# Sliding-window attention with slot experts: keys in blocks of 64 that meet 96 queries, TensorE in program order

## The chip, the cores and the metric

The kernel runs on one core of a Trainium2 chip. The metric is the device time of one execution in microseconds; the median over runs is compared. A core has five engines that run their own queues side by side: TensorE (matmuls, with weight loads that overlap them), VectorE, ScalarE, GpSimd and SyncE. Here GpSimd and SyncE do little but issue DMA transfers. PSUM is the matmuls' output memory, eight banks of 2 KB for each of 128 partitions.

## The reference

Attention over 8 batches, 8 heads, 576 positions and 64 dimensions; four heads see the last 32 positions, four see every fourth of the last 128. The result, as 4608 rows of 512, goes through a soft mixture of 8 experts with 4 slots each.

```python
scores = scale * np.matmul(q, k.transpose(0, 1, 3, 2))
rel = pos[:, None] - pos[None, :]
mask_plain = (rel >= 0) & (rel < 32)
mask_dil = (rel >= 0) & (rel < 128) & (rel % 4 == 0)
attn = softmax(np.where(masks, scores, -1e9))
x = np.matmul(attn, v)                      # -> [4608, 512]
logits = x @ phi                            # [4608, 32]
slot_input = softmax(logits, axis=0).T @ x  # over all rows
for e in range(8):
    slot_out[e] = np.maximum(slot_input[e] @ w1[e], 0.0) @ w2[e]
out = softmax(logits, axis=1) @ slot_out
```

The softmax over all rows means that no expert can start before the last batch's attention is done.

## The kernel before

The work is cut into 32 units: batch `b` and a pair of heads, four units a batch in the order plain, dilated, plain, dilated (`unit`). A unit goes through these stages.

- `transposes` turns q and k (96 rows by 64 columns at a time, on TensorE) and copies them out of PSUM, on ScalarE into `qT` (two buffers) and `kTp`, on VectorE into `kTd` for the dilated units.
- `scores` multiplies 128 keys by 160 queries (plain) or 128 keys by 144 queries and 16 more (dilated), two heads on the two halves of the contracted rows, in two parts with a PSUM tile of two banks each.
- `softmax_parts` applies exp on ScalarE, one instruction for each part, and multiplies by a 0/1 mask on VectorE. There is no subtraction of a maximum; a column of ones in V gives the sum.
- `values` multiplies the masked exp with V, in two halves of three and two output blocks; VectorE takes a reciprocal of the sums (L399) and scales (L400) for each half.
- `x_transposes` turns the result into `xT` for the logits.

Once a batch, `select_v` (L205, L216, L225) uses matmuls with 0/1 matrices (`pick`) to bring the loaded V from "four rows to a partition" to one row to a partition; ScalarE copies the result to `vp`. `spread_v` (L194) copies the dilated V into `vd`, on VectorE. `front_logits`, `front_rows` and `front_slots` follow a batch, five to seven units later, with the logits, the exponentials by rows, and the slot sums. `last_early`, `last_logits` and `last_slots` do the last batch. Then `expert_in` (L675, ReLU L683, transposes L686) and `expert_out` (L699) take experts in pairs, `so` is copied, and eleven output tiles are computed (L735) and stored from SyncE's queue.

Loads: SyncE's queue takes the first part of q, the identity, the masks and phi; GpSimd's takes all q, k and v, converted from fp32 to fp16 on the way (`load_batch`, seven transfers a batch, all eight batches in a row), then w1 and w2 of each expert into the memory where a batch's q, k and v lay (`home0` to `home7`). So w1 of expert `e` waits until batch `e` has been read out.

Order: tiles and dependencies are tracked by a framework that orders each engine's queue by its own estimate when the program is built; only GpSimd's queue is kept as written. At run time each engine's queue is strictly in order. The calls stand like this:

```python
for u in range(NU + 5):
    st = scores(u + 1)
    values(u)
    softmax_parts(u + 1, st)
    transposes(u + 3)
    ...  # front_*, by u % 4
    x_transposes(u - 1)
    if u % 4 == 3: spread_v(u // 4 + 1); select_v(u // 4 + 1)
```

Of the kernel before, what the change touches and what calls it, by code (L numbers as in the profile page):

```python
# [15 lines left out]
B = 8  # L16
# [16 lines left out]
QW = 160  # L33
# [3 lines left out]
DW = CL + 16  # L37
# [6 lines left out]
def constants():  # L44
    j = np.arange(128)[:, None]
    i = np.arange(QW)[None, :]
    d = i - j
    keep = ((d >= 0) & (d < WINDOW)).astype(np.float16)
    m, n = np.arange(128)[:, None], np.arange(64)[None, :]
    ends = (m // 32 == n // 16) & (m % 32 <= n % 16)  # L50
    band = np.concatenate([keep, ends], axis=1).astype(np.float16)
    ident = np.eye(128, dtype=np.float16)
    return band, ident
# [3 lines left out]
def kernel(  # L57
# [11 lines left out]
    band_np, ident_np = constants()  # L69
    band_dram = nc.inline_tensor(band_np, name="band_d")  # L70
    ident_dram = nc.inline_tensor(ident_np, name="ident_d")

    consts = ctx.enter_context(tc.tile_pool(name="consts", bufs=1))
    ident = consts.tile([128, 128], FP16, name="ident")
    mask = consts.tile([128, QW + 2 * N_SLOTS + 256], FP16, name="mask")
    phi_sb = consts.tile([128, 4, N_SLOTS], FP32, name="phi_sb")
# [5 lines left out]
    nc.sync.dma_start(out=ident, in_=ident_dram.ap())  # L82
    nc.sync.dma_start(out=mask[:, 0 : QW + 64], in_=band_dram.ap())
    nc.sync.dma_start(out=phi_sb, in_=moe_phi.rearrange("(p r) s -> p r s", r=4))
# [13 lines left out]
    pick = kept([128, 4, 32, 4], "pick")  # L98
# [15 lines left out]
    Pp = kept([128, 2, NKB, 256], "Pp")  # L114
    P1 = kept([128, 2, 4, 128], "P1")
    P2 = kept([128, 2, 4, 2, 32], "P2")
# [7 lines left out]
    nc.vector.memset(Pp[:, :, :, QW:], 0.0)  # L124

    nc.vector.memset(Pp[:, :, 4, 64:QW], 0.0)
    nc.vector.memset(Pp[0:1, :, 4, 64:128], 1.0)
    nc.vector.memset(P2, 0.0)
    nc.vector.memset(P2[0:1, :, :, 0, 16:32], 1.0)
    for i in range(2):  # L130
        nc.vector.memset(vd[i][:, :, D : D + 1], 1.0)
    for i in range(NV):
# [4 lines left out]
    qT_pool = ctx.enter_context(tc.tile_pool(name="qT", bufs=2))  # L137
# [8 lines left out]
    ring = ctx.enter_context(  # L146
        tc.tile_pool(name="ring", bufs=2, space=bass.MemoryType.PSUM)
    )
    ps_o = tc.alloc_tile_pool(name="ps_o", bufs=2, space=bass.MemoryType.PSUM)
    ps_s = tc.alloc_tile_pool(name="ps_s", bufs=2, space=bass.MemoryType.PSUM)  # L150
# [3 lines left out]
    def load_batch(b):  # L154
# [15 lines left out]
        for nm, ten, hs, rows in (  # L170
# [14 lines left out]
            if nm == "kp":  # L185
                if b == 0:
                    nc.gpsimd.dma_start(out=rest[0], in_=rest[1])  # L187
                load_v("vp", 0, 4, 0, t[:, 6144:7168])
                load_v("vt", 0, 8, 512, t[96:112, 0:2048])
        load_v("vd", 4, 4, 0, t[:, 7168:8192])  # L190
# [7 lines left out]
    def select_v(b):  # L198
        raw, last = raws[b]["vp"], raws[b]["vt"]
        for i in range(2):  # L200
            sel = ps_s.tile([128, 2, 2, 4, D], FP32, name=f"sel{b}_{i}", tag="s")
            for r in range(4):
                for n in range(2):
                    rows = slice(64 * i + 32 * n, 64 * i + 32 * n + 32)
                    nc.tensor.matmul(  # L205
                        sel[:, n, 0],
                        pick[rows, r].rearrange("p i j -> p (i j)"),
                        raw[rows, :, r, :],
                        start=(r == 0),
                        stop=(r == 3),  # L210
                        tile_position=(64 * i + 32 * n, 0),
                    )
            nc.scalar.copy(out=vp[b % NV][:, 2 * i : 2 * i + 2, :, 0:D], in_=sel[:, :, 0])  # L213
        end = ring.tile([128, 2, 4, D], FP32, name=f"sel{b}_2", tag="ring")
        for r in range(4):
            nc.tensor.matmul(  # L216
                end[:, 0],
                pick[96:112, r].rearrange("p i j -> p (i j)"),
                last[:, 0:4, r, :],
                start=(r == 0),  # L220
                stop=(r == 3),
                tile_position=(96, 0),
            )
        for r in range(4):
            nc.tensor.matmul(  # L225
                end[32 * r : 32 * r + 32, 1],
                ident[96:112, 96:128],
                last[:, 4:8, r, :],
                start=True,
                stop=True,  # L230
                tile_position=(96, 32 * r),
                skip_group_check=True,
            )
        nc.scalar.copy(out=vp[b % NV][:, 4:6, :, 0:D], in_=end)
# [26 lines left out]
    def transposes(u):  # L261
        b, hp = unit(u)
        for nm in ("q", "k"):
            if nm == "q":
                dst = qT_pool.tile([128, S], FP16, name=f"qT{u}", tag="qT")
                qTs[u] = dst
            else:
                dst = kTp if hp < 2 else kTd
                kTs[u] = dst
# [30 lines left out]
    def scores(u):  # L300
        b, hp = unit(u)
        qT, kT = qTs[u], kTs[u]
        tiles = []
        for part in range(2):
            st = ps_s.tile([128, 2, 512], FP32, name=f"s{u}_{part}", tag="s")
            if hp < 2:
                todo = [(160 * i, 128 * i, 128 * i, QW) for i in range(3)] if part == 0 else [
                    (0, 384, 384, QW), (QW, 512, 512, 64)]
            else:
                todo = [(DW * cc, CL * (2 * cc + part), CL * (2 * cc + part), CL) for cc in range(2)]  # L310
                todo += [(DW * cc + CL, None, CL * (2 * cc + part) + 128, 16) for cc in range(2)]
            for at, k0, q0, n in todo:
                for g in range(2):
                    ks = q0 - 32 * g - 64 * (at // DW) if k0 is None else k0
                    nc.tensor.matmul(  # L315
                        st[:, g, at : at + n],
                        kT[64 * g : 64 * g + 64, ks : ks + 128],
                        qT[64 * g : 64 * g + 64, q0 : q0 + n],
                        start=True,
                        stop=True,  # L320
                    )
            tiles.append(st)
        return tiles

    def softmax_parts(u, tiles):
        b, hp = unit(u)
        for part in range(2):
            st = tiles[part]
            if hp < 2:
                n = (480, 224)[part]  # L330
                pr = raw_pool.tile([128, 2, n], FP16, name=f"pr{u}_{part}", tag=f"pr{part}")
                nc.scalar.activation(out=pr, in_=st[:, :, 0:n], func=AF.Exp, scale=SCALE)  # L332
                for b0, nb, w in ((0, 3, QW),) if part == 0 else ((3, 1, QW), (4, 1, 64)):
                    at = (b0 - 3 * part) * QW
                    nc.vector.tensor_tensor(  # L335
                        out=Pp[:, :, b0 : b0 + nb, 0:w],
                        in0=pr[:, :, at : at + nb * w].rearrange("p h (t c) -> p h t c", c=w),
                        in1=mask[:, None, None, 0:w].broadcast_to([128, 2, nb, w]),
                        op=ALU.mult,
                    )  # L340
                continue
            if part == 0:
                pr = dil_pool.tile([128, 2, 2, 2, DW], FP16, name=f"pd{u}", tag="pd")
            nc.scalar.activation(  # L344
                out=pr[:, part].rearrange("p c e t -> p e c t"),
                in_=st[:, :, 0 : 2 * DW].rearrange("p e (c t) -> p e c t", c=2),
                func=AF.Exp,
                scale=SCALE,
            )
        if hp < 2:  # L350
            return
        pr = pr.rearrange("p a c e t -> p a (c e) t")
        nc.vector.tensor_tensor(
            out=P1.rearrange("p a c t -> p (a c) t"),
            in0=pr[:, :, :, 0:128].rearrange("p a c t -> p (a c) t"),
            in1=mask[:, None, 0:128].broadcast_to([128, 8, 128]),
# [3 lines left out]
        nc.vector.tensor_tensor(  # L360
            out=P2.rearrange("p a c s t -> p (a c) s t")[:, :, :, 0:16],
            in0=pr[:, :, :, 128:DW].rearrange("p a c (s t) -> p (a c) s t", s=2),
            in1=mask[:, QW + 64 :].rearrange("p (c s t) -> p c s t", c=8, s=2),
            op=ALU.mult,
        )

    def values(u):
# [7 lines left out]
        for half in range(2):  # L375
            blocks = (0, 1, 2) if half == 0 else (3, 4)
            nb = len(blocks)
            ot = ps_o.tile([128, 3, 2, D + 1], FP32, name=f"o{u}_{half}", tag="o")
            mms = []
            for i, blk in enumerate(blocks):  # L380
                for h in range(2):
                    if plain:
                        P, vt = Pp, vp[b % NV]
                        mms.append((ot[:, i, h], P[:, h, blk, 0:128], vt[:, blk, hl + h, :]))
                        if blk > 0:
# [395 lines left out]
```

## Time and profile before

| | |
|---|---|
| median of 3 runs | 185.69 us (185.67 to 186.18) |
| span of the profiled execution | 183.5 us |
| TensorE busy | 151.8 us, 83% of the span |
| VectorE, ScalarE busy | 117.1 us (64%), 115.5 us (63%) |
| software DMA queue (GpSimd's) | 30.79 MB written, 93.9% of 16 engines' span |
| last weights landed | 156.74 us |
| output stored | from 158.9 us to the end |

The profile is of one execution. Busy time of an engine is the union of its instructions' times; a matmul's time includes its way through the array, so several overlap. A line of the timeline gives start, duration, engine, source line, operation, output and inputs, shapes, count, and in brackets how long the engine sat idle before it and what ended that. The clock of TensorE is recorded from 39.0 us on: full until 138.0, half until 148.2, full until 168.7, then half.

### The profile page before, as it was taken

The numbers are of one execution on the slowest core, as the hardware profiler recorded it, in microseconds if no ns is written. First come the engines' busy times: TensorE is split into PE (matmuls) and PEld (weight loads), VectorE is DVE, ScalarE is ACT, GpSimd is POOL, SyncE is SP. The second block draws the span as 40 slices with busy tenths as digits, with TensorE's granted clock in tenths as the row PEclk, the third lists the DMA queues.
The fourth block names the chain that finished last, engine by engine and source line by source line (L and its number), as shares of the span: only waits on it lengthen the run. The fifth ranks groups of instructions, "written<-read, shape, count | busy, mean of one in ns | idle before, by whom it ended". The sixth has DMA issues, their size and how long they took to land.

```text
span 183.5 us, 6054 instructions
## 1 busy us (share of the span) xinstructions
PE 151.8 (83%) x2595; PEld 105.8 (58%) x2595; DVE 117.1 (64%) x363; ACT 115.5 (63%) x208; POOL 46.9 (26%) x77
## 2 busy tenths in 40 slices
PE   1869999999988989998997998898979998885300
PEld 1637776677676667666765767666768644432000
DVE  7605886388877877878779687786970111496410
ACT  2248845689599789779878959977703022675410
POOL 7752555464554654401102001003100000000000
PEclk9999999999999999999999999999995589998555
DMA  5999999999999999999999999999999995199996
GB/s 103 183 203 203 202 203 201 202 202 204 204 201 201 204 199 204 226 211 221 212 216 216 212 216 216 218 212 218 218 214 220 212 208 105 75 440 427 427 427 262
DMA packets 23978, 41.06 MB, mean 224 GB/s; under 512 B 1680, under 2 KB 20240, under 8 KB 21136
## 3 DMA queue, kind: packets, MB, share of 16 engines
q0 software_dynamic: 21584, 30.79, 93.9%
q1 hardware_dynamic: 2368, 9.89, 13.4%
q8 instruction: 20, 0.33, 0.6%
q14 instruction: 6, 0.05, 0.1%
HBM read 62.02 MB, written 9.44 MB: 389 GB/s over the span
## 4 chain that ended last, share of the span: by engine, by line
DMA 74%; issue 15%; POOL 3%; ACT 2%; DVE 1%; PE 0%; POOLq 0%; DVEq 0%; SPq 0%
DMA home<-in_moe_w_dram 31%; DMA home<-in_v_dram 15%; DMA home<-in_k_dram 12%; DMA home<-in_q_dram 9%; DMA out_dram<-ot 7%; ACT ot L739 2%; DVE ot L741 1%; POOL home L250 1%; POOL home L162 1%; POOL home L239 1%; POOL home L184 0%; POOL home L187 0%; ACT so L716 0%; PE sop L699 0%; PE f L735 0%
## 5 line engine op out<-in xcount | busy, mean ns | idle before, releaser
L400 DVE TENSOR_TENSOR x<-o,rc 128x384 f16<-128x384 f32 x64 | 29.9, 482 | 0.5
L332 ACT ACTIVATE pr<-s 128x960 f16<-128x960 f32 (+1 forms) x32 | 24.7, 780 | 1.8 <-PE s L315 1.8
L344 ACT ACTIVATE pd<-s 128x640 f16<-128x640 f32 x32 | 20.9, 706 | 1.7 <-PE s L315 1.7
L162 POOL DMA_DIRECT2D home<-in_v_dram x24 | 16.6, 692 | 16.6 <-DMA home<-in_k_dram 11.6
L205 PE MATMUL sel<-home,pick 32*128 32x256 f16 x128 | 17.8, 307 | 1.4 <-DMA home<-in_v_dram 1.1
L399 DVE RECIPROCAL rc<-o 128x6 f32<-128x6 f32 x64 | 10.2, 177 | 13.5 <-PE o L395 13.4
L416 PE MATMUL rgx<-ident,x 128*128 128x128 f16 x160 | 15.6, 233 | 3.0 <-ACT qT L295 3.0
L741 DVE TENSOR_SCALAR ot<-f,rrow 128x512 f32<-128x512 f32 (+1 forms) x19 | 12.5, 716 | 7.7 <-DMA out_dram<-ot 5.2
L335 DVE TENSOR_TENSOR Pp<-pr,mask 128x960 f16<-128x960 f16 (+2 forms) x48 | 16.4, 394 | 0.4 <-ACT pr L332 0.4
L280 ACT COPY qT<-rgq 128x576 f16<-128x576 f16 x16 | 10.3, 641 | 9.0 <-PE rgq L275 8.5
L422 ACT COPY xT<-rgx 128x512 f16<-128x512 f16 x16 | 9.6, 601 | 10.0 <-PE rgx L416 10.0
L739 ACT ACTIVATE ot<-f,rrow 128x512 f32<-128x512 f32 (+1 forms) x19 | 11.2, 675 | 7.0 <-DMA out_dram<-ot 6.6
L239 POOL DMA_DIRECT2D home<-in_moe_w_dram x8 | 4.3, 534 | 44.4 <-PE rgq L290 36.5
L213 ACT CAST vp<-sel 128x512 f16<-128x512 f32 x16 | 9.4, 590 | 9.2 <-PE sel L205 9.0
L416 PEld LDWEIGHTS <-x 128*128 128x128 f16 x160 | 10.2, 102 | 7.2 <-issue 5.4
L735 PE MATMUL f<-so,ET 128*128 128x512 f16 (+1 forms) x38 | 11.0, 402 | 3.9 <-ACT ot L739 3.0
L275 PEld LDWEIGHTS <-home 96*64 96x64 f16 x384 | 11.9, 123 | 3.9 <-issue 2.0
L184 POOL DMA_DIRECT2D home<-in_k_dram x16 | 10.6, 661 | 10.1 <-DMA home<-in_q_dram 8.2
L395 PE MATMUL o<-vp,Pp 128*128 128x65 f16 x288 | 12.9, 203 | 0.0
L436 PE MATMUL l<-xT,phi 128*128 128x288 f16 x64 | 10.8, 304 | 2.0 <-ACT qT L280 1.7
L295 DVE COPY kTd<-rgk 128x576 f16<-128x576 f16 x16 | 12.0, 752 | 0.6 <-PE rgk L290 0.5
L295 ACT COPY qT<-rgq 128x576 f16<-128x576 f16 x16 | 10.3, 646 | 3.1 <-PE rgq L290 2.6
(105 smaller groups left out, 292.9 us busy)
## 6 DMA issues: line engine op xcount, KB each, us to landing
home<-in_moe_w_dram POOLq DMA_DIRECT2D x15, 1024.0 KB, 30.1
out_dram<-ot SPq DMA_DIRECT2D x7, 1024.0 KB, 7.5
home<-in_k_dram POOLq DMA_DIRECT2D x16, 288.0 KB, 9.9
home<-in_q_dram POOLq DMA_DIRECT2D x15, 288.0 KB, 9.7
home<-in_v_dram POOLq DMA_DIRECT2D x16, 256.0 KB, 9.8
out_dram<-ot SPq DMA_DIRECT2D x3, 512.0 KB, 6.5
home<-in_moe_w_dram POOLq DMA_DIRECT2D x2, 512.0 KB, 27.3
home<-in_v_dram POOLq DMA_DIRECT2D x8, 64.0 KB, 8.9
```

Of the source, the lines that this page charges most:

```text
L162: nc.gpsimd.dma_start(out=dst, in_=v[b, h0 : h0 + n_h, r0 : r0 + 4 * n_p, :].rearrange("h (p r) d -> p h (r d)", r=4),)
L205: nc.tensor.matmul(sel[:, n, 0], pick[rows, r].rearrange("p i j -> p (i j)"), raw[rows, :, r, :], start=(r == 0), stop=(r == 3), tile_posi ...
L275: nc.tensor.transpose(rg[64 * h : 64 * h + 64, r, :], raw[:, 2 * hp + h, D * r : D * r + D], ident[0:NP, 0:NP],)
L295: (nc.scalar.copy if nm == "q" else nc.vector.tensor_copy)(out=dst[:, 0:S].rearrange("c (g p a) -> c g p a", g=4, a=3), in_=rg.rearrange(" ...
L332: nc.scalar.activation(out=pr, in_=st[:, :, 0:n], func=AF.Exp, scale=SCALE)
L335: nc.vector.tensor_tensor(out=Pp[:, :, b0 : b0 + nb, 0:w], in0=pr[:, :, at : at + nb * w].rearrange("p h (t c) -> p h t c", c=w), in1=mask ...
L344: nc.scalar.activation(out=pr[:, part].rearrange("p c e t -> p e c t"), in_=st[:, :, 0 : 2 * DW].rearrange("p e (c t) -> p e c t", c=2), f ...
L395: nc.tensor.matmul(to, lhs, rhs, start=(n == 0), stop=(n == len(mms) - 1), skip_group_check=True)
L400: nc.vector.tensor_tensor(out=x[:, blocks[0] : blocks[0] + nb, D * hl : D * hl + 2 * D].rearrange("p t (h d) -> p t h d", h=2), in0=ot[:, ...
L416: nc.tensor.transpose(rg[:, 128 * blk : 128 * blk + 128], x[:, blk, hl : hl + 128], ident)
L739: nc.scalar.activation(out=ot[:, j, d0:d1], in_=fp, func=AF.Copy, scale=scale)
L741: nc.vector.tensor_scalar(out=ot[:, j, d0:d1], in0=fp, scalar1=scale, scalar2=None, op0=ALU.mult)
```

## The change

Keys come in blocks of 64: the lower and the upper half of the partitions hold two key blocks, and each meets 96 queries. All scores of a unit lie in one PSUM tile, one exp covers them, and one mask product (two for dilated units) follows. Values are multiplied from half the rows at a time, a block of the lower half of one head beside a block of the upper half of the other; the second half of them is moved behind the x transposes of the unit before, and waits for the first through an empty instruction on SyncE's queue. One reciprocal and one scaling cover a unit. q has one buffer each for plain and dilated units; scores and output have one PSUM tile each, and the shared `ring` has four banks, not two. `select_v` contracts over 64 rows with zeros in `pick`; its last block becomes `select_ends`, which is called two units later. TensorE's queue is kept as written, like GpSimd's, and the driver loop is rearranged; `spread_v` and `select_v` of the next batch are called in the first unit of a batch, not the last. Identity and masks are one constant with one load, and phi is loaded through GpSimd's queue behind batch 0. `expert_in` of the next pair comes ahead of the turn of the present one.

```diff
+    fixed = consts.tile([128, 128 + TAIL + QW + 4 * TAIL], FP16, name="fixed")
+    ident, mask = fixed[:, 0:128], fixed[:, 128:]
+    phi_sb = consts.tile([128, 4, N_SLOTS], FP16, name="phi_sb")
-    nc.sync.dma_start(out=ident, in_=ident_dram.ap())
-    nc.sync.dma_start(out=mask[:, 0 : QW + 64], in_=band_dram.ap())
-    nc.sync.dma_start(out=phi_sb, in_=moe_phi.rearrange("(p r) s -> p r s", r=4))
+    nc.sync.dma_start(out=fixed, in_=fixed_dram.ap())
...
     def select_v(b):
+        raw = raws[b]["vp"]
+        sel = [ring.tile([128, 2, 4, D], FP32, name=f"sel{b}_{i}", tag="ring") for i in range(2)]
+        for n in range(2):
+            for r in range(4):
+                for i, part in enumerate((LOW, UP)):
+                    nc.tensor.matmul(
+                        sel[i][:, n],
+                        pick[part, n, r].rearrange("p i j -> p (i j)"),
+                        raw[part, :, r, :],
...
+    def select_ends(b):
+        last = raws[b]["vt"]
+        end = ring.tile([128, 2, 4, D], FP32, name=f"end{b}", tag="ring")
         for r in range(4):
             nc.tensor.matmul(
+                end.rearrange("p a h d -> p (a h) d"),
+                pick_end[64:112, r],
+                last[:, :, r, :],
...
     def scores(u):
+        st = ps_s.tile([128, 2, 512], FP32, name=f"s{u}", tag="s")
...
+        if hp < 2:
+            for blk in range(NKB):
+                for g in range(2):
+                    for s, rows in enumerate((LOW, UP)):
+                        k0 = 128 * blk + HB * s
+                        score(rows, g, QW * blk, k0, min(k0, S - HB), QW)
+            return st
+        for i in range(4):
+            for g in range(2):
+                score(LOW, g, QW * i, CL * i, CL * i, QW)
+                score(UP, g, QW * i, CL * i + HB, CL * (i + 1) - QW, QW)
+        for i in range(4):
+            for g in range(2):
+                q0 = CL * i + 128
+                c = 2 * (i // 2) + g
+                score(slice(0, 128), g, 4 * QW + TAIL * i, q0 - HB - TAIL * c, q0, TAIL)
...
+    def softmax_parts(u, st):
+        n = NKB * QW if hp < 2 else 4 * (QW + TAIL)
+        nc.scalar.activation(out=pr, in_=st[:, :, 0:n], func=AF.Exp, scale=SCALE)
...
     def values(u):
+        ot = ps_o.tile([128, 2, 512], FP32, name=f"o{u}", tag="o")
...
+        def rest():
+            first = pairs((0, up[0]), (1, low[1]))[0]
+            tc.add_manual_dep(first, fence.name, after, reason="the other row tile is through")
+            run(tails)
+            normalise(u, ot, x, hl)
+
+        before = pairs((0, low[0]), (1, up[1]))[1]
+        fence = nc.sync.nop(nofuse=True).ins
+        tc.add_manual_dep(fence, before.name, after, reason="this row tile is through")
+        later[u] = rest
...
+    def select(u):
+        b = u // 4 + 1
+        if b < B and u % 4 == 0:
+            spread_v(b)
+            select_v(b)
+        elif b < B and u % 4 == 2:
+            select_ends(b)
...
-    ctx.enter_context(tc.manual_schedule(engines={mybir.EngineType.Pool}))
+    ctx.enter_context(
+        tc.manual_schedule(engines={mybir.EngineType.Pool, mybir.EngineType.PE})
+    )
     for b in range(B):
         load_batch(b)
+        if b == 0:
+            nc.gpsimd.dma_start(out=phi_sb, in_=moe_phi.rearrange("(p r) s -> p r s", r=4))
     spread_constants()
     transposes(0)
     spread_masks()
+    softmax_parts(0, scores(0))
+    transposes(2)
+    select_v(0)
+    select_ends(0)
     spread_v(0)
     transposes(1)
-    select_v(0)
-    st = scores(0)
-    softmax_parts(0, st)
-    transposes(2)
     for u in range(NU + 5):
         if u + 1 < NU:
+            softmax_parts(u + 1, scores(u + 1))
+        if 0 < u and u + 3 < NU:
             transposes(u + 3)
...
+        front(u)
+        select(u)
+        if u < NU:
+            values(u)
+        if u == 0:
+            transposes(3)
+            spread_phi()
         if 0 <= u - 1 < NU:
             x_transposes(u - 1)
+        if u < NU:
+            later[u]()
...
+    expert_in(0)
     for pr in range(4):
-        expert_in(pr)
-        if pr >= 1:
-            expert_out(2 * pr - 2)
-            expert_out(2 * pr - 1)
+        if pr < 3:
+            expert_in(pr + 1)
+        expert_turn(pr)
+        if pr < 3:
+            expert_out(2 * pr)
+            expert_out(2 * pr + 1)
```

In the driver loop, unit 0 was followed by scores of unit 1 and its own values at once; now the order of a pass is scores, transposes, `front`, `select`, values, x transposes, and the rest of the values.

## The prediction, made before the changed kernel had run

> **What bounds the kernel now.** I read the page first, then the chain of waits in order of time, the timeline at both ends, and engine sums by stage.
>
> ```profile
> span 183.5 us, 6054 instructions
> ...
> DMA  5999999999999999999999999999999995199996
> ...
> DMA 74%; issue 15%; POOL 3%; ACT 2%; DVE 1%; PE 0%; POOLq 0%; DVEq 0%; SPq 0%
> ```
>
> The DMA engines are busy to about 152 us (slice 33 of 40), pause, and then write the output. The chain that ended last is three quarters DMA: one unbroken stream on GpSimd's queue.
>
> ```profile
> 126.91 0.53 POOL L239 DMA_DIRECT2D home<-in_moe_w_dram  x1 [14.42 <-PE rgq L290]
> ...
> 155.81 0.54 PEld L699 LDWEIGHTS <-hTp 128*32 128x32 f16 x13 [0.22 <-DVE hTp L691]
> 156.79 0.10 PEld L699 LDWEIGHTS <-hTp 128*32 128x32 f16 x3 [0.44 <-issue]
> ```
> ```profile
> 128.48 28.27 DMA home<-in_moe_w_dram
> 156.74 0.04 issue
> 156.78 0.42 PE sop L699 x4
> ```
>
> The last half of w2[7] lands at 156.74 and four matmuls go at once. But TensorE waited only 0.44 us for it: attention, last softmax and experts end almost level with the stream. So nothing that only speeds up the attention can win much, and whatever delays it by more than 0.44 us is paid in full. The fence's first line shows how far the stream itself can bear a delay: the last four transfers (3 MB at the page's 215 GB/s, 14.6 us) begin near 142.1, and the first of them was issued at 126.91, some 15 us ahead.
>
> ```profile
> 12.96 0.78 POOL L162 DMA_DIRECT2D home<-in_v_dram  x1 [0.76 <-DMA home<-in_k_dram]
> 14.04 0.43 DVE L194 COPY vd<-home 128x1024 f16<-128x1024 f16 x1 [4.93 <-DMA home<-in_v_dram]
> 14.38 0.75 DVE L295 COPY kTd<-rgk 128x576 f16<-128x576 f16 x1
> 16.05 0.46 PE L315 MATMUL s<-qT,kTd 64*128 64x144 f16 x8
> 18.23 0.20 DVE L399 RECIPROCAL rc<-o 128x6 f32<-128x6 f32 x1 [1.46 <-PE o L395]
> ...
> 24.16 0.68 POOL L184 DMA_DIRECT2D home<-in_q_dram  x1 [0.56 <-DMA home<-in_v_dram]
> ```
>
> The beginning: unit 0 reaches its reciprocal at 18.23. GpSimd's queue holds eight transfers in flight; the issue at 24.16 waited for the one eight before it, issued at 12.96: batch 1's dilated V, landed near 23.9 (the chain shows 0.28 us from landing to issue).
>
> ```profile
> 95.00:115.00 20.00, 17.85 (x404) 13.62 (x404) 15.65 (x48) 16.98 (x32) 1.59 (x3) 1.00 1.03 215
> ```
>
> In the steady stage (columns: TensorE, its weight loads, VectorE, ScalarE, GpSimd, clock, DMA share, GB/s), summed over 35 to 135 us, TensorE is busy 92%, ScalarE 82%, VectorE 80%. A batch takes 15.04 us (reciprocals of equal place at 96.24 and 126.32, two batches apart): 13.8, 12.3 and 12.0 us of work.
>
> **The change, part by part.**
>
> *Start.* In the new program VectorE's queue has batch 1's copy of dilated V (`spread_v(1)`, called in the loop's first pass) ahead of unit 1's `kTd` copy. VectorE stands at it until the landing: 23.9, plus 0.3 for phi, which is now ahead in the queue (64 KB; at 200 to 400 GB/s 0.16 to 0.3, taken at the upper end). Then 0.43 for that copy and 0.75 for `kTd`: 25.4. TensorE, now in program order, has unit 1's scores next, and behind them everything: selection of batch 1, unit 0's values, transposes of unit 3, phi. At the slow clock of this stage (65-column matmuls 56 ns apart, 18 in 1.17 us at 35.8, against 30 after 39.0): 24 score matmuls at 46 ns 1.1; 8 selection pairs of 256 columns at 0.22 1.75; 13 value matmuls 0.75; 12 transposes 1.1; 8 phi matmuls at 0.1 0.85; 13 values 0.75. That is 6.3; unit 0's reciprocal comes near 31.8 instead of 18.2: **+13.6**. If the VectorE copy did not hold TensorE, the selection would still wait for batch 1's plain V (landed by 19.6): about 24.9, +6.7, the lower bound.
>
> *First units.* Five units after unit 0 took 21.9 us before (reciprocals 18.2 to 40.1), nearly all at the slow clock. I take the same: 0. Bounds: 17.8 at the later pace (-4.1), 24 if the extra mode changes are paid at slow clock (+2).
>
> *Steady pace.* TensorE per batch: scores are four 64x64 tiles side by side, 96 columns at 41 ns per four (six 96-column transposes in 0.42 us, one lasting 0.22, start 40 ns apart). Plain 0.34 (four pairs at 77 ns, a short one) to 0.21, dilated 0.40 to 0.31, twice each -0.4. Values: 16 steps of paired half-height tiles at 33 ns are as long as 18 at 30; dilated 0.50 to 0.40; being split around the x transposes they change tile shape twice more per unit, 0.1 each (30 against 123 ns from 128- to 32-wide tiles): +0.6. Selection 8 pairs as before; its last block 4 matmuls of 512 columns at 0.215 instead of 8 short ones of about 0.55 together: +0.3. So TensorE's work is not less: 13.8 + 0.4 = 14.2. ScalarE: one exp of 960 (0.99) for 0.99 + 0.57, and one of 896 (about 0.94, by that slope) for two of 0.71: -2.1. VectorE: one mask product of 960 for three, one normalisation of 640 (about 0.81 and 0.23) for two: -2.6. With both lighter, I let TensorE's present idle 1.2 us vanish: 14.2 per batch, -0.84; over the 6.5 batches (26 units) from 40.1 to 134.3, **-5.5**. Bounds: 13.0 (less overlap in TensorE's busy record than I count; -13), 15.6 (as now plus the added work and a little waiting; +4). Single buffers for scores, output and q, and the fence through SP's queue (nothing but the final output is behind it there), lie behind five x transposes (0.43), the k and q transposes (0.66) and selection or logits; uncovered, each costs some 0.1 to 0.2 a unit, which is in the upper bound.
>
> *End.* Program order puts all eight last logits matmuls between the slot sums and the experts; before, two stood there (0.24 apart at the slow clock): +1.45. Experts with the next input product ahead of the turn lose the 0.84 us wait for the first ReLU; the 0.44 us wait for the last weights goes too: **+0.2** together.
>
> *Loads.* phi behind batch 0's loads, the single constant for identity and masks, and about a fifth more TensorE instructions to fetch (page: 20 packets on the instruction queue, 0.6% of 16 engines' span, 0.88 us each; about four more) push the stream's end by 0.3 to 1 us. The late computation covers it: 0; without that cover +0.3.
>
> Sum: 13.6 + 0 - 5.5 + 0.2 = 8.3 on this execution's span of 183.5, or, span to median 2.2 apart, 185.7 + 8.3 = **194.0**.
>
> **The rivals.**
>
> *The stream stays the bound (not slower).* All of the late start is won back: 13.6 must be met by the pace, 2.1 us a batch, so from a batch of 13.0 us on. For it: ScalarE and VectorE fall to near 10 us a batch. Against: TensorE's own 13.8. Then 185.7 + 0.3 = 186.0, between 185.0 (the start's transfers shrink from 384 small packets to 256) and 186.7.
>
> *The clock comes early.* Selection and unit 3's transposes now stand in one solid stretch after 26 us; if the full clock is granted there, not some 20 us later, the five first units take 17.8: 189.9. Against: before, TensorE was busy 19.6 of 20 us from 15 to 35 and still ran slow. [...]
>
> *No gain in pace.* TensorE in a fixed order waits as often as it does now, and a batch stays at 15.04: 185.7 + 13.6 + 0.2 = 199.5; with a batch of 15.6, 203.
>
> *The halves do not run side by side.* Then scores, values and selection cost some 3.6 us a batch more: 194.0 + 6.5 x 3.6 = 217. Against: sixteen score matmuls of a dilated unit fit into 0.51 us now, though one lasts 0.17 to 0.24.
>
> **How the numbers follow.** Forecast 0.33 (191 to 197), early clock 0.20, no gain 0.20, stream 0.22, no pairing 0.05. I call 0.3% (0.56 us) what a measurement can tell from no change. The stream case splits into faster 0.08, same 0.12, slower 0.02; all others are slower: 0.08, 0.12, 0.80. The range, 185.7 to 202, leaves out most of the faster part, no pairing, and the worst of no gain.
>
> **What would show it.** In the changed profile: VectorE's copy of dilated V waiting near 24 for a load, with TensorE idle from about 16 to 25; the first `rc` near 32; equal reciprocals two batches apart 28.4 us apart; w1[7] issued near 135; the chain that ended last running through TensorE, ScalarE and VectorE in the middle instead of loads; and no wait at the last `sop` matmuls. I am wrong if the last expert matmuls still wait for a landing near 157, or if the first reciprocal comes before 25.

## The result: 13% slower, most of it in the middle

The changed kernel takes 212.20 us (median of 4, 210.07 to 215.81) where the kernel before takes 185.68 (185.40 to 186.18): a ratio of 1.132, 95% interval 1.126 to 1.139. The forecast was 194.0 with a range of 185.7 to 202. The direction was right; the size was not. Executions of one kernel spread by up to 5% in this study, with the granted clock: medians and ranges are of all of them, a ratio compares those within 1.5% of each kernel's fastest, and none is given where only one lies there.

From the page of the kernel after: the span, the TensorE clock and the DMA share in 40 slices, the instruction queue, and the shares of the chain that ended last.

```profile
span 209.1 us, 6998 instructions
...
PEclk9999999997598557859985965595797559999855
DMA  6999999999999999999999999960289900069996
...
q8 instruction: 24, 0.39, 0.7%
...
PE 58%; DMA 14%; DVE 13%; issue 6%; ACT 3%; POOL 2%; DVEq 0%; ACTq 0%; SPq 0%; POOLq 0%
```

The chain is no longer the load stream: TensorE holds 58% of it and VectorE 13%. The clock, full from 39.0 to 138.0 us before, now falls to a half again and again. The last weights land at 168.3; the last `sop` matmuls (from 181.13) do not wait for them.

The timeline at the start (start us, length us, engine, line, in brackets the idle time ahead and what ended it):

```profile
14.23 0.43 DVE L198 COPY vd<-home 128x1024 f16<-128x1024 f16 x1 [4.14 <-DMA home<-in_v_dram]
...
23.21 0.43 DVE L198 COPY vd<-home 128x1024 f16<-128x1024 f16 x1 [5.43 <-DMA home<-in_v_dram]
23.55 0.75 DVE L290 COPY kTd<-rgk 128x576 f16<-128x576 f16 x1
24.36 0.74 PE L302 MATMUL s<-qTd,kTd 64*64 64x96 f16 x24 [8.58 <-DVE kTd L290]
...
29.83 0.21 DVE L424 RECIPROCAL rc<-o 128x10 f32<-128x10 f32 x1
```

This is the late start as forecast: batch 1's copy of dilated V holds VectorE until its load lands, `kTd` stands behind it, and TensorE has nothing for 8.58 us.

Sums of 50 to 130 us (length, then busy time and count of TensorE, its weight loads, VectorE, ScalarE, GpSimd; clock, DMA share, GB/s), first of the kernel before, then of the kernel after:

```profile
50.00:130.00 80.00, 73.08 (x1539) 54.55 (x1535) 63.71 (x192) 66.69 (x124) 18.43 (x31) 1.00 1.12 212
```
```profile
50.00:130.00 80.00, 70.20 (x1518) 51.29 (x1517) 46.49 (x106) 45.15 (x81) 16.09 (x27) 0.73 1.12 212
```

As many matmuls as before in the same 80 us, though a batch now has 351 of them instead of 287 (counted between reciprocals of equal place). VectorE and ScalarE are idler, TensorE no busier, the clock 0.73 instead of 1.00.

Split at the first reciprocal (`rc`) of units 0, 5 and 31, the difference of the two spans is:

| stretch | before | after | difference | forecast |
|---|---|---|---|---|
| start to unit 0 | 18.2 | 29.8 | +11.6 | +13.6 |
| unit 0 to unit 5 | 21.9 | 17.9 | -4.0 | 0 |
| unit 5 to unit 31 | 94.2 | 112.4 | +18.2 | -5.5 |
| unit 31 to the end | 49.2 | 49.0 | -0.2 | +0.2 |
| sum | 183.5 | 209.1 | +25.6 | +8.3 |

So the third row is to be explained most of all: 112.4 us, of which 55.6 at half clock.

### The profile page after: what moved, and what is told of

Same layout as the page of the kernel before. It is cut to its first block, busy times and chain, and to the rows that moved or that the text cites. A ratio compares the mean times of both kernels' runs of the same rounds, so it can differ in the third digit from the quotient of the medians.

```text
span 209.1 us, 6998 instructions
## 1 busy us (share of the span) xinstructions
PE 158.3 (76%) x3111; PEld 111.0 (53%) x3111; DVE 111.0 (53%) x280; ACT 100.5 (48%) x176; POOL 47.7 (23%) x78
## 3 DMA queue, kind: packets, MB, share of 16 engines
q1 hardware_dynamic: 2080, 9.81, 11.6%
## 4 chain that ended last, share of the span: by engine, by line
PE 58%; DMA 14%; DVE 13%; issue 6%; ACT 3%; POOL 2%; DVEq 0%; ACTq 0%; SPq 0%; POOLq 0%
PE o L399 12%; DMA home<-in_v_dram 8%; PE rgx L441 7%; DMA out_dram<-ot 6%; PE s L302 5%; PE sel L208 5%; PE l L465 5%; DVE x L425 4%; PE end L223 3%; PE rgq L270 3%; DVE kTd L290 2%; PE h L730 2%; PE u L518 2%; PE rgk L270 2%; PE rgq L285 2%
## 5 line engine op out<-in xcount | busy, mean ns | idle before, releaser
L425 DVE TENSOR_TENSOR x<-o,rc 128x640 f16<-128x640 f32 x32 | 26.3, 822 | 0.6
L399 PE MATMUL o<-vp,Pp 64*128 64x65 f16 x416 | 22.4, 212 | 0.4 <-issue 0.3
L424 DVE RECIPROCAL rc<-o 128x10 f32<-128x10 f32 x32 | 7.0, 219 | 28.8 <-PE o L399 28.5
L165 POOL DMA_DIRECT2D home<-in_v_dram x24 | 16.8, 702 | 17.0 <-DMA home<-in_k_dram 10.9
L399 PEld LDWEIGHTS <-Pp 64*128 64x128 f16 x416 | 15.6, 108 | 6.9 <-issue 4.6
L441 PE MATMUL rgx<-fixed,x 128*128 128x128 f16 x160 | 17.7, 254 | 0.0
L399 PE MATMUL o<-vd,Pd 64*128 64x65 f16 (+1 forms) x384 | 14.5, 207 | 2.1 <-DVE x L425 1.5
L302 PE MATMUL s<-qTd,kTd 64*64 64x96 f16 (+1 forms) x384 | 9.6, 208 | 8.6 <-DVE kTd L290 8.6
L399 PEld LDWEIGHTS <-Pd 64*128 64x128 f16 (+1 forms) x384 | 8.9, 101 | 11.7 <-issue 4.7
L223 PE MATMUL end<-home,pick_end 48*128 48x512 f16 x32 | 13.3, 560 | 0.0
L275 ACT COPY qTp<-rgq 128x576 f16<-128x576 f16 x16 | 10.3, 642 | 6.2 <-PE rgq L270 6.2
L270 PEld LDWEIGHTS <-home 96*64 96x64 f16 x384 | 12.4, 137 | 1.5 <-DVE pick_end L601 0.2
## 6 DMA issues: line engine op xcount, KB each, us to landing
home<-in_moe_w_dram POOLq DMA_DIRECT2D x2, 512.0 KB, 15.6
```

Source lines behind the costliest of these rows:

```text
L165: nc.gpsimd.dma_start(out=dst, in_=v[b, h0 : h0 + n_h, r0 : r0 + 4 * n_p, :].rearrange("h (p r) d -> p h (r d)", r=4),)
L223: nc.tensor.matmul(end.rearrange("p a h d -> p (a h) d"), pick_end[64:112, r], last[:, :, r, :], start=(r == 0), stop=(r == 3),)
L270: nc.tensor.transpose(rg[64 * h : 64 * h + 64, r, :], raw[:, 2 * hp + h, D * r : D * r + D], ident[0:NP, 0:NP],)
L302: nc.tensor.matmul(st[rows, g, at : at + n], kT[half, k0 : k0 + rows.stop - rows.start], qT[half, q0 : q0 + n], start=True, stop=True, ski ...
L399: nc.tensor.matmul(to, lhs, rhs, start=(h not in begun), stop=True, skip_group_check=True)
L425: nc.vector.tensor_tensor(out=x[:, :, D * hl : D * hl + 2 * D].rearrange("p t (h d) -> p h t d", h=2), in0=o[:, :, :, 0:D], in1=rc[:, :, : ...
```

## The experiments

**What stands out in the trace.** Three things in the steady stage of the kernel after. First, once a batch, TensorE stands at the quarter matmuls (L504). The timeline of one such place:

```profile
66.77 0.59 PE L486 MATMUL e<-fixed,ET 128*128 128x32 f16 x13
66.97 0.76 DVE L290 COPY kTd<-rgk 128x576 f16<-128x576 f16 x1 [1.73 <-PE rgk L285]
67.64 0.55 DVE L343 TENSOR_TENSOR Pd<-pr,mask_d 128x768 f16<-128x768 f16 x1
68.11 0.22 DVE L349 TENSOR_TENSOR Pt<-pr,mask_t 128x128 f16<-128x128 f16 x1
68.24 0.48 DVE L502 CAST Er<-e 128x320 f16<-128x320 f32 x1
68.78 0.27 PE L504 MATMUL e<-quarter,ET 128*128 128x1 f16 x4 [1.42 <-DVE Er L502]
```

The row matmuls (L486) and the quarter matmuls write one PSUM tile, and VectorE's copy `Er` between them is fourth in VectorE's queue. In program order TensorE stands there: 1.65 us from one start to the next, 10.9 us over seven batches.

Second, gaps 0.5 to 2.4 us long (from one matmul's start to the next), always between matmul number 94 and 95 counted modulo 128 from the first; the profile finds no semaphore that ended them, but for one of the larger ones, which it puts down to ScalarE. 128 matmuls with their weight loads are 256 instructions. The packets on the instruction queue are 16,384 bytes each, 24 of them now for 6222 matmuls and weight loads and 20 before for 5190, about 259 to a packet both times, and each such gap ends 1.25 to 1.5 us after one. The kernel before has no such gap.

Third, the clock falls and returns in steps of 3.413 us: the 15 stretches at full or half clock ahead of the last one take 2 to 7 times that, the three in the kernel before 29, 3 and 6 times. The runs below take these apart. All times stand against the kernel before on the same chip: 185.52 for the first four, 185.91 for the next four, 185.55 for the next three and 185.80 for the last two.

**The quarter matmuls at the end of the pass**

```diff
         ep = ring.tile([128, 11, N_SLOTS], FP32, name=f"e{b}", tag="ring")
...
+        return ep, cols
+
+    def front_sums(ep, cols):
         for n, (_, c0, nj) in enumerate(cols):
             nc.tensor.matmul(
...
+        if sums:
+            front_sums(*sums)
```

> Only the small matmuls that sum the rows (quarter) are moved in TensorE's order, from right behind the row matmuls to the end of the pass, so that TensorE no longer stands 1.65 us a batch (9.5 us in all) for VectorE's Er copy. Waits alone: the 9.5 us come back, 201 to 203. Clock theory (a wait thins TensorE's work, the granted clock falls to half for two to four windows of 3.4 us): the waits and most of the half-clock stretches come back, 194 to 199, and the share of half clock between 30 and 150 us falls from some 45% to below 25%. Instruction-fetch theory (TensorE gets 128 matmuls per 16 KB fetch, about 6 us each): 207 to 211, with longer idle stretches that end on nothing.

Measured: 207.76 (204.47 to 209.73), ratio 1.108 [1.100, 1.116]. The median lies in the 207 to 211 of the fetch theory, the two fastest executions (204.47, 205.90) in none of the three ranges. The waits are gone. Unit 5 to 31 takes 108.1 instead of 112.4 us. What they had cost came back in part as gaps of the second kind: 16 us of them where the kernel after has 8, both counted from start to start. One of them, TensorE's timeline:

```profile
110.23 0.42 PE L285 MATMUL rgk<-fixed,home 96*128 96x96 f16 x6
110.58 0.39 PE L208 MATMUL sel<-home,pick 64*128 64x256 f16 x3
113.19 1.65 PE L208 MATMUL sel<-home,pick 64*128 64x256 f16 x13 [2.21 <-issue]
```

TensorE stops in the middle of a row of equal matmuls whose data and tile are there. Over two batches late in this run (98 to 132 us) a batch takes 16.65 us for 351 matmuls, 6.07 us for 128.

**Batch 1's copy of dilated V behind unit 0**

```diff
-            spread_v(b)
             select_v(b)
         elif b < B and u % 4 == 2:
             select_ends(b)
+            spread_v(b)
...
+        if b == 1:
+            tc.add_manual_dep(copy.ins, done[0].name, after, reason="behind unit 0")
```

> Only batch 1's copy of dilated V is held behind unit 0's reciprocal in VectorE's queue. Unit 1's scores then start near 17 instead of 24.4, selection of batch 1 waits for its plain V (18.7), unit 0's reciprocal comes near 24.5 instead of 29.8. Start theory: 5 us come back, 205 to 207. If what follows is bound by something else that a start of 5 us does not move (the clock, fetch), the time stays at 209 to 212.

The edit does a little more than that: every batch's copy of dilated V is now called two units later, not only batch 1's. Measured: 208.53 (207.94 to 210.47), ratio 1.128 [1.120, 1.135], between the two expectations. The first `rc` comes at 24.5 instead of 29.8, the last at 157.5 instead of 160.1: of 5.3 us won, 2.6 are left 31 units later. The waits at the quarter matmuls are as they were, and half clock lasts 57.7 us between units 5 and 31 (55.6).

**Work in the wait, and its control.** Seven matmuls of 512 columns whose result nobody reads (identity against `phi4`) fill the wait at L504, by estimate 1.5 us of it (the 512-column matmuls of the output tiles start 0.216 us apart at full clock in the kernel after). They need a PSUM bank, so the ring has three instead of four; the control has three and no filler.

```diff
             nc.vector.tensor_copy(out=Er[b % 2], in_=ep[:, 0:10])
+            for _ in range(7):
+                nc.tensor.matmul(
+                    spare, ident, phi4.rearrange("p a b s -> p (a b s)"), start=True, stop=True
+                )
```

> Ring of three banks, and seven matmuls of 512 columns into a bank of their own stand between the row matmuls and the sums, in the place where TensorE waits 1.65 us a batch (1.5 us at full clock). Nothing is waited less. Waits alone and fetch theory: the time of the ring-3 control, or up to 5 us more. Clock theory: TensorE's work no longer thins, half clock falls below 20% of the stretch from 30 to 150 us, and it is 5 to 12 us faster than the ring-3 control.

> Control for the next kernel: the shared ring has three banks instead of four. All theories: 211 to 216, a little slower for a few waits on banks.

Measured: filler 208.60 (207.28 to 209.59), ratio 1.124 [1.117, 1.132]; control 213.75 (208.45 to 215.93). Nothing is waited for less, yet in the profiled executions (209.59 and 214.18) unit 5 to 31 takes 110.6 us against 116.5, with 20.5 us of half clock against 59.5. The clock rows of the two pages, filler first:

```profile
PEclk9999999969998787999996589699999559999555
```
```profile
PEclk9999999996559579969965975566697559999855
```

Useless work brought clock back: the mean granted clock of the four executions is 0.84 to 0.91 with the filler and 0.78 to 0.84 in the control. That it also made the kernel faster is not shown, since one execution of the control took 208.45, inside the filler's own range.

**Both repairs, and the framework's order.** First the two edits above together; then the kernel after with one line changed, TensorE left to the framework's scheduler as before the change.

```diff
-        tc.manual_schedule(engines={mybir.EngineType.Pool, mybir.EngineType.PE})
+        tc.manual_schedule(engines={mybir.EngineType.Pool})
```

> Both edits together: the quarter matmuls at the end of the pass, and batch 1's copy of dilated V behind unit 0's reciprocal. First rc near 24.5, no waits at the quarter matmuls. If TensorE is held by the arrival of its instructions, one block of 128 matmuls per 6 us or so, the earlier start is kept whole and the pace of the steady stage stays that of the run with the first edit alone (128 us from the first rc to the last): 207.8 - 5 = 203. If instead the granted clock balances the work over the kernel, what is won at the start is lost again to more half clock, as with the second edit alone: 205 to 207. If the prediction's only faults were these two waits, 194.

> The changed kernel with TensorE's order left to the framework's scheduler (GpSimd alone in program order), as before the change. If the order written out by hand is what cost the time (the quarter matmuls beside Er, the start), TensorE finds other work at those places: no wait over 0.5 us at them, about 194. If the number of instructions (3111 matmuls against 2595) and the thinner tiles are the cost, the time stays near 205 to 208, with stalls at matmul numbers 94 modulo 128 and half clock in a third of the steady stage.

Measured: both repairs 199.91 (198.57 to 203.44), ratio 1.074 [1.066, 1.081]; framework's order 200.05 (198.19 to 202.35), ratio 1.069 [1.061, 1.077]. Two quite different orders without the waits at L504 meet at the same time: unit 5 to 31 is 108.1 and 108.6 us. Framework's order has 15.5 us of the gaps at 94 modulo 128 and 16.60 us a batch over the same two batches as above, 6.06 us for 128 matmuls; both repairs take 16.18 there, 5.90 for 128. Neither run met an expectation: both repairs were to take 203, 205 to 207 or 194, the framework's order 194 or 205 to 208. So the order as it was written by hand costs about 12 us of the 26; the other 14 remain in both of these orders.

**Without the weight loads.** Experts 1 to 7 use the weights of expert 0, so that no loads run from about 87 us on; once on the run with the quarter matmuls moved, once on the kernel after as it is.

```diff
     def load_w1(e):
+        if e > 0:
+            w_tiles[e] = w_tiles[0]
+            return
...
     def load_w2(e):
+        if e > 0:
+            return
```

> The run with the quarter matmuls moved, and one expert's weights only: experts 1 to 7 use those of expert 0, and 14 MB of loads are left out, so the DMA engines have nothing but instructions to move from about 80 us to the output. If the stalls are instruction fetches that are slow behind the saturated load stream, there is none after 85 us, the clock stays full, and the 18 units left then take near 3.1 us each: last rc near 143 (159.2 with all loads), 190 in all. If a stall at every block is a property of TensorE's fetch whatever the loads do, the stalls stay and the last rc comes at 157 to 160, 204 to 207 in all. If the stalls only follow the clock, the same 204 to 207.

> The changed kernel as it is, with one expert's weights only (experts 1 to 7 use those of expert 0; 14 MB of loads are left out). Its quarter matmuls still wait 1.65 us for VectorE each batch. If fetches behind the load stream are what stalls TensorE, the stalls after 85 us go (2.2 us of them before), and what they cost in clock: 203 to 207. If the waits at the quarter matmuls alone make the clock fall, half clock returns in every batch in the same windows and the time is 208 to 211. If the loads cost nothing, 210 to 212.

Measured: 187.69 (187.59 to 187.80) with the quarter matmuls moved, and 211.43 (205.14 to 215.28) without. Sums of 85 to 135 us, columns as above: the moved quarter matmuls with all loads, the same without loads, and the kernel after without loads:

```profile
85.00:135.00 50.00, 42.57 (x1109) 32.50 (x1110) 32.25 (x75) 33.03 (x62) 2.64 (x5) 0.93 1.03 216
```
```profile
85.00:135.00 50.00, 48.55 (x1397) 37.38 (x1391) 42.46 (x102) 39.47 (x72) 0.00 (x0) 1.00 0.02 5
```
```profile
85.00:135.00 50.00, 45.98 (x960) 33.89 (x960) 29.49 (x68) 27.82 (x50) 0.00 (x0) 0.69 0.01 3
```

From the first row to the second only the loads are taken away: 1109 matmuls become 1397, DMA share 1.03 becomes 0.02. Four gaps over 0.4 us at 94 modulo 128 lie before, the last at 62.8 us (7.3 us together), and none after; instruction packets come 3.3 to 5.2 us apart instead of about 6, and a batch takes 12.4 us at full clock. The place of the gaps, the packets just before their ends and their absence without loads all say the same: the gaps are TensorE waiting for its own instructions, which arrive too late behind a load stream of 216 GB/s at a DMA share of 1.03. The third row has neither loads nor such gaps, but the waits at L504, and its clock is 0.69 where the second row has 1.00: here 1.65 us of standing in each batch was enough to lose the clock, and the half clock took far more than the wait itself. The first run came out faster than the expected 190. The second was expected at 203 to 207: its median is no better than with all loads (212.20), but its fastest execution, 205.14, lies in that range.

**Fewer matmuls for the same result.** On the run with both repairs, the mask step writes the low half of a slot at column 0 and the high half where it was, so that the first value product of both halves is one matmul over 128 rows: 319 matmuls a batch instead of 351, two VectorE instructions instead of one.

```diff
-                    low[h].append((to[t], Pp[LOW, h, t, HB:SLOT], vn[LOW, t, hl + h, :]))
...
-                    up[h].append((to[t], flat[:, SLOT * t : SLOT * t + 128], vn[UP, t, hl + h, :]))
+                    whole.append((h, (to[t], Pp[:, h, t, 0:128], vn[:, t, hl + h, :])))
```

> As the run with both edits, and the first value product of each pair of half blocks as one matmul over all 128 rows: VectorE's mask step writes the low half at column 0 of its slot and the high half where it was, in two instructions (2.4 us more of VectorE a batch), so that both meet the same 128 queries. 319 matmuls a batch instead of 351, 2855 in all; the same result. If the pace is what the fetch allows (128 matmuls per 6.07 us behind the loads, the figure of the run with the first edit), a batch takes 15.1 us instead of 16.6, and the time falls from 199.9 to 188 or 190. If the pace is TensorE's own work, nothing changes there (the paired halves ran side by side): 199 to 201. If VectorE becomes the bound: 202 or more.

Measured: 193.72 (191.83 to 197.66), ratio 1.039 [1.030, 1.048]. Six of the ten to twelve us came. The gaps shrank to 4 us, but a batch took 16.6 (unit 4 to unit 28), not 15.1: the clock was at a half for 49.1 us between units 5 and 31 (in the profiled execution, 197.66).

**The count alone, in the kernel before.** Each score matmul of the kernel before is preceded by a one-column copy of itself (52 more a batch), with all loads and with one expert's.

```diff
                     ks = q0 - 32 * g - 64 * (at // DW) if k0 is None else k0
+                    nc.tensor.matmul(
+                        st[:, g, at : at + 1],
+                        kT[64 * g : 64 * g + 64, ks : ks + 128],
+                        qT[64 * g : 64 * g + 64, q0 : q0 + 1],
+                        start=True,
+                        stop=True,
+                    )
```

> The kernel before, with each score matmul preceded by a one-column copy of itself: 52 matmuls more a batch (339 instead of 287), 416 in all, same result. If TensorE is fed 128 matmuls per 6.07 us behind the loads, a batch cannot be shorter than 16.1 us (14.99 without them): gaps of 1 to 2.5 us at matmul number 94 modulo 128 show up in this kernel too, which had none, and with them half clock; 193 or more. If only their own work counts (52 at some 35 ns, 1.8 us in a batch with 1.2 us to spare), no such gap, full clock, 186 to 191.

> The same with one expert's weights only (experts 1 to 7 use those of expert 0; 14 MB of loads are left out). If the fetch is slow only behind the loads, no gap at 94 modulo 128 after 85 us, full clock from there, and a batch of 15 to 16 us; before 85 us gaps as in the run with all loads. If the gaps come from the number of matmuls alone, they go on to the end of the attention.

Measured: 210.10 (204.88 to 213.49) with all loads, 213.05 (207.55 to 213.84) without. Both theories missed. At 94 modulo 128 there is one gap of 0.89 us and no row of them, and nothing is won without the loads. But 52 one-column matmuls a batch made the kernel 24 us slower by the medians (20 by the fastest executions, 204.88 and 184.72). In the profiled execution, the one of 204.88, full clock was granted at 20.5 us and then lost for 58.0 us before the last unit was through; the kernel before got it at 39.0 and did not lose it until 138.0, after its last reciprocal.

**Idle time or array use?** Two runs that add work nobody needs: the run with whole-row products plus three filler matmuls of 512 columns a unit, and the kernel before with each score matmul done twice at full width instead of the one-column copy.

```diff
+        if 0 < u < NU:
+            spare = ring.tile([128, 512], FP32, name=f"spare{u}", tag="ring")
+            for _ in range(3):
+                nc.tensor.matmul(
+                    spare, ident, phi4.rearrange("p a b s -> p (a b s)"), start=True, stop=True
+                )
```
```diff
-                    nc.tensor.matmul(
-                        st[:, g, at : at + n],
...
+                    for _ in range(2):
+                        nc.tensor.matmul(
+                            st[:, g, at : at + n],
```

> The run with whole-row value products, plus three matmuls a unit whose result nobody reads (identity against 512 columns of phi, 0.65 us of TensorE's time a unit at full clock, 12 matmuls a batch: 331). If the clock follows how much of the array a window of 3.413 us uses, the windows that lost it with 2250 to 2500 columns' worth of full array rise above 3500, half clock falls from 49 us to under 20 us of the stretch from the first rc to the last, and in spite of the added work a batch comes to 15.7 us, what the fetch allows: 186 to 189 in all, against 193.7. If the clock follows waits or stalls, these stay and the fillers' time is added: 196 to 204.

> The kernel before with each score matmul run twice at its full width, instead of once at one column and once in full: as many matmuls (3011), but 64 to 160 columns where there was one; same result. TensorE's own work per batch grows by 1 us more. If array use sets the clock, it stays full nearly throughout, and a batch takes 16 to 17 us: 194 to 200, faster than with the one-column copies (210). If the number of matmuls or their work is what costs, it is slower than those: 211 or more.

Measured: 187.67 (186.72 to 189.30), ratio 1.011 [1.004, 1.018], for the full copies; 194.00 (193.20 to 199.75), ratio 1.042 [1.037, 1.047], for the filler. Sums of 50 to 130 us of the kernel before with one-column copies, then with full copies:

```profile
50.00:130.00 80.00, 76.63 (x1489) 57.99 (x1485) 52.02 (x157) 54.82 (x100) 16.25 (x27) 0.76 1.12 212
```
```profile
50.00:130.00 80.00, 74.22 (x1687) 58.59 (x1684) 58.66 (x178) 61.68 (x115) 16.31 (x27) 1.00 1.12 212
```

Both kernels have 3011 matmuls. The one whose copies are thin keeps TensorE busier (76.63 of 80 us) and gets a clock of 0.76; the one that does more work gets 1.00 and is 22 us faster by the medians, 18 by the fastest executions. Matmuls take longer at half clock (those of 128x128 at L441 of the kernel after start 106 ns apart, 56 at full clock), so the share of busy time alone proves little; but window by window it comes out the same way. Of the windows of 3.413 us at full clock between 30 and 150 us, the six after which the kernel with thin copies lost it had TensorE busy for 2.8 to 3.2 us, while the kernel before kept its clock after windows with 2.46 and 2.41 us (from 52.7 and 97.0). So in these runs the clock is lost not with idle time as such, but where little of the array is used. The time is also below the 194 to 200 expected: a batch takes 16.1 us, the last `rc` comes at 138.3 (134.3 before the edit), and the load stream, whose last weights land at 156.8, still covers it. The same rows of the run with whole-row products, then with the filler (its profiled execution was the one of 199.75):

```profile
50.00:130.00 80.00, 76.81 (x1512) 55.74 (x1510) 60.55 (x132) 50.30 (x91) 17.20 (x28) 0.75 1.12 212
```
```profile
50.00:130.00 80.00, 76.60 (x1597) 53.68 (x1593) 63.23 (x136) 51.73 (x94) 17.09 (x28) 0.97 1.12 212
```

The clock came back (0.75 to 0.97) as expected, but the time did not follow: 194.00 is not the 186 to 189 expected, and the fillers take as much as the clock gives. Up to 119 us a batch takes 15.7 us in the mean (15.1 to 16.9), the 15.7 worked out from 331 matmuls at 6.07 us per 128. Whether it is the fetch or TensorE's own work, filler included, that sets this pace stays open.

## Why the prediction was wrong, point by point

**Start: right mechanism, 11.6 instead of 13.6.** The copy waited as said, the copy began at 23.21 instead of 24.2, and the work behind it took 5.5 us from the scores to the first reciprocal, not the 6.3 of my sum (which would have ended at 31.7, not the 31.8 written). With the copy moved away 5.3 us came back at unit 0.

**First units: the rival "the clock comes early" came true here, and only here.** Full clock was granted at 29.4 us and five units took 17.9 us, close to the 17.8 I had put as the lower bound. I gave 0.20 to that case and expected it to last.

**Steady pace: the step that failed.** I summed TensorE's work at full clock to 14.2 us a batch and took the clock and the supply of instructions for given; 18.0 was measured (unit 4 to unit 28, six batches). My terms for the added work make +0.5, not the +0.4 written, which hardly matters beside that. The work itself was, if anything, overestimated: with no loads, no wait at L504 and full clock a batch takes 12.4. What I left out, by the runs:

- The wait at L504. I had costed the order by hand as mode changes and had not looked for two groups of matmuls on one PSUM tile with a VectorE copy between them. Taking it out is worth 4.3 us between units 5 and 31 with all loads, and, with the loads taken away, 24 us by the medians (211.43 to 187.69) and 18 by the fastest executions (205.14 to 187.59).
- The fetch. I had counted the added packets in "Loads", but as load on the DMA queues, not as something TensorE waits for. In the twelve profiled kernels with all loads only 4 of 193 intervals between these packets (30 to 140 us) are shorter than 5.8 us. At 5.8 to 6.07 us per 128, 351 matmuls take 15.9 to 16.6 us a batch, and over two batches in a row no run with 351 and all loads took less than 16.2; the kernel before, with 287, would meet that limit at 13.0 to 13.6 and runs at 15.0. This alone speaks against 14.2.
- The clock. From the matmuls' shapes in the trace, columns times the share of the array's rows and columns in use, a batch is 17,000 full-array columns in both kernels. At 15.0 us a batch that is 3,900 in a window of 3.413 us, at 18.0 it is 3,200. The change thinned nothing over a batch; but anything that stretches a batch thins its windows, windows below some 2,870 lose the clock by the fit given in the last section, and the lost clock stretches the batch further.

How the 14 us that are not the order divide between the fetch and the clock stays open: no run keeps the loads and takes away the late instructions alone.

The rival "no gain in pace" (199.5, up to 203) had the right sign and still assumed full clock. The rival "the halves do not run side by side" (217) came nearest in size, for a reason that did not hold: at 12.4 us a batch they must run side by side.

**Loads.** Right that the late computation covers them: no wait at the last `sop`. **End:** -0.2 against +0.2.

**Range.** Its upper end came from a batch of at most 15.6 us. Beyond that only the missing pairing was priced, although the change adds 64 matmuls to a batch; the profile of before did not show by itself how close it ran to the two limits.

## What to carry to other kernels

A pace for TensorE that is summed from durations at full clock holds only if the clock is still full at the new pace: here 14.2 us a batch were summed, and 18.0 measured at a mean clock of 0.73 (50 to 130 us). Work out the array use of each window (3.413 us here), and if waits or thin tiles bring it near the lowest one that held before (2,892 columns here), cost the stretch at half clock too. Count instructions as well as columns: here two half-size matmuls in place of one ran side by side, at 12.4 us a batch without loads, and still arrived too late behind them, at 16.2 us a batch or more. When an engine is put in program order, look for each place where it writes a tile that another engine reads in between (here L504, 1.65 us a batch).

## What the hardware showed that was not expected

**The clock followed array use, window by window.** Over the windows between 30 and 157 us of all 15 profiled kernels, one bound, chosen on these same windows, says whether the next window runs at full clock: 2,870 full-array columns in 3.413 us. It is right for 508 of 547 windows, and for 343 of the 354 that ran at full clock (always saying "full" would be right for 279 of these); the misses lie between 2,692 and 3,272. The rivals do worse with the best bound on the same 547 windows: TensorE's busy time is right for 395, columns that are not weighted with the share of the array for 443. In the kernel before the lowest windows of the steady stage had 2,892, 2,964 and 3,012, and held; in the kernel after full-clock windows of 1,705 to 3,029 were followed by half clock. It is a fit, not a mechanism that was shown; the runs with full copies and with the filler were expected from it, and their clock came out so. An idle window was not needed: with one-column copies TensorE was busy for 2.8 us or more of each of the six windows after which it lost the clock.

**Late instructions stalled TensorE.** Behind loads at 212 to 216 GB/s the gaps at 94 modulo 128 lasted up to 2.35 us in the kernel after, from start to start, and three kernels with no wait at the quarter matmuls came to 6.07, 6.06 and 5.90 us per 128 matmuls over the same two batches; without loads the first of these programs went through 128 in 4.5 us with no gap. Why the gap falls behind matmul 94 of 128 was not tried, and the full copies, which at 6.0 to 6.2 us per 128 show hardly a gap, leave open whether that pace is the fetch's or their own.
